# Bucketed attention, a gated feed-forward and routed experts on one core: a smaller set of sign projections, wider evictions and a new order of all lists

## The chip, the cores and the metric

The kernel runs on one core of one Trainium2 chip. The metric is the device time in microseconds (us) of one launch. The engines are named as the profile names them: PE is TensorE's matmul, PEld its weight load, DVE VectorE, ACT ScalarE, POOL GpSimd, SP the engine that issues most DMAs.

## What is computed

Three parts follow each other; the output of one is the input of the next, 768 tokens by 512.

```python
# 1. attention, 8 heads, 768 tokens, 64 wide; six sign bits put a token in a bucket
q_bits = (q @ proj) > 0 ; k_bits = (k @ proj) > 0          # proj: 64 x 6
mask   = bucket(q_bits)[:, None] == bucket(k_bits)[None, :]
scores = where(mask, q @ k.T / 8, -1e9)
attn   = exp(scores - max) ; attn /= attn.sum() + 1e-9
x      = attn @ v
# 2. gated feed-forward with a product over tokens
h      = gelu(x @ w_in)                                     # 512 -> 1024
u, v   = h[:, :512], h[:, 512:]
v_s    = w_sg @ (layernorm(v) * g_ln) + b_sg[:, None]       # 768 x 768 over tokens
x      = x + (u * v_s) @ w_out
# 3. eight experts; a token keeps the expert of the token before it when a gate says so
e      = sticky_argmax(x @ w_gate, x @ w_local)
out[s] = p[e] * (relu(x[s] @ w1[e]) @ w2[e])
```

## The kernel before

All matrices are split into a high part (fp32r) and a low part, and a product is the sum of high x high, high x low and low x high. The kernel is written as one program whose order on PE, DVE, ACT, POOL and SP is set by hand: four texts (`ATTENTION`, `FEED_FORWARD`, `MIXING`, `EXPERTS`) list steps such as `score 2 3` (head 2, tile 3), and each step issues its instructions on its engines in that order. An engine works through its own instructions in order and waits on semaphores for the others.

**Attention.** For each head h, `load_head` brings q and k (transposed, each twice, on partitions 0 to 63 and 64 to 127). `prep` makes the operands of 768 columns: k1 (high part of k), k2 (low part on partitions 0 to 63, key bits at 64 to 75), q1 (high part of q above, low part below), q2 (high part of q, query bits). `project` multiplies the sign projections into one PSUM bank for the keys and one for the queries, four matmuls each over two halves of 384 columns, eight a head (L404), and `bits` compares them with thresholds (L411, L413). `score` makes a tile of 128 x 768 scores in four matmuls (L420, L423), `row_max` reduces it on DVE (L427), `numerators` takes the exponential on ACT (L431), `turn` transposes three blocks of 128 x 128 on PE into a bank (L437), `evict` copies these 384 columns to SBUF on ACT (L443), `pv` multiplies them with the values (L453). `mean_part`, `to_x`, `sum_v` and the low parts of q and k use POOL. The operands of head h + 2 and the bits of head h + 1 are made while head h is scored.

**w_in and w_out** arrive as 64-bit floats and are taken apart on chip: `f64_chunks` is a generator, and each list step `conv` runs the next of its eight parts for a chunk of 128 x 512: a load on SP, a `lift` on ACT, four integer or scalar operations on DVE (L281 to L294), an addition on POOL (L273), a cast (L300), a subtraction on POOL (L273). Eight chunks are w_in's, four are w_out's; all twelve are converted beside attention.

**Feed-forward and mixing.** `hv` and `h` are the products with w_in (L314); for each token tile follow `sq`, `cub`, `tanh`, `gelu`, and for the half that is normalised `dev`, `z`, `var`, `norm`, `vh`, `vl`. `wsg` loads (L732), casts (ACT, L735) and splits (POOL, L737) a tile of w_sg, `mix` is the product over tokens (L744), `gated` and `gT` prepare its result, `out` is the product with w_out (L767), `res` adds x. PSUM buffers for `h`, `mix` and `out` come from a pool of four, taken in turn. `route` is a generator of some twenty small DVE steps for a token tile, with `what_all` (L868) among its last; its key goes through a transpose on PE (L822). `gx` and `fill` gather the tokens of the experts by matmul.

**Experts.** `wr` reads a quarter of one weight matrix of an expert (SP, L647), `wh` casts it (ACT, L655), `wl` splits off its low part (L661, on POOL for the parts in `ON_POOL`, else on DVE). `f`, `relu`, `ht`, `y` are an expert's two products, `yo` weighs the rows, `send` scatters them.

## Time and profile before

| | us | share of the span |
|---|---|---|
| median of 3 runs (346.26 to 347.0) | 346.53 | |
| the profiled execution | 347.04 | |
| its span, first to last instruction | 344.6 | |
| PE busy, 1860 matmuls | 327.5 | 95% |
| PEld busy, 1860 weight loads | 256.8 | 75% |
| DVE busy, 516 instructions | 272.5 | 79% |
| ACT busy, 432 | 233.9 | 68% |
| POOL busy, 162 | 203.5 | 59% |

The stages lie at about 0 to 12 us (start), 12 to 144 (attention), 144 to 178 (feed-forward and the first mixing products), 178 to 240 (mixing, output, routing), 240 to 338 (experts) and the end. Busy time is a sum over stages with different limits, and the end of a matmul is modelled in the profile; what a change is worth is read in its stage, from the steps between starts and from the waits.

### The profile page before, as it was taken

What the parts mean: (1) busy time and instruction counts of PE and PEld (TensorE: products, weight loads), DVE (VectorE), ACT (ScalarE), POOL (GpSimd) and SP (SyncE); (2) the same over time, 40 slices, a digit from 0 to 9 for tenths busy, and PEclk for the clock granted to TensorE, in tenths of its full rate; (3) what the DMA queues carried; (4) which work ended last, traced back from release to release, by engine and by line L of the source; (5) the groups of instructions that cost most, each with busy time, mean ns of one, the idle gap of its engine ahead of it and who ended that gap; (6) DMA issues with size and microseconds to landing.
All of it is one profiled execution on the core that took longest, in us unless ns stands there. A gap on an engine that the chain in (4) does not pass through costs nothing.

```text
span 344.6 us, 5450 instructions
## 1 busy us (share of the span) xinstructions
PE 327.5 (95%) x1860; PEld 256.8 (75%) x1860; DVE 272.5 (79%) x516; ACT 233.9 (68%) x432; POOL 203.5 (59%) x162
## 2 busy tenths in 40 slices
PE   7899999999999999999989999879999999999992
PEld 6787777667777657788767776559888888788892
DVE  4899999989998865788753768988589868798933
ACT  3589888888888775299455364364659786869540
POOL 3378867688858645247434674865732674574651
PEclk9999999999999999999999999998999999999997
DMA  6914043213421024011107429292979979999510
GB/s 248 331 45 153 3 152 121 92 38 119 133 82 61 10 62 132 0 57 52 46 7 253 124 89 327 81 357 66 343 252 303 336 288 368 348 330 364 216 60 32
DMA packets 25951, 55.82 MB, mean 162 GB/s; under 512 B 2878, under 2 KB 7486, under 8 KB 25920
## 3 DMA queue, kind: packets, MB, share of 16 engines
q1 hardware_dynamic: 23872, 50.67, 42.7%
q0 software_dynamic: 1120, 3.15, 2.7%
q10 hardware_dynamic: 928, 1.62, 1.4%
q8 instruction: 16, 0.26, 0.3%
q14 instruction: 15, 0.12, 0.1%
HBM read 52.28 MB, written 3.67 MB: 162 GB/s over the span
## 4 chain that ended last, share of the span: by engine, by line
PE 73%; DVE 13%; DMA 4%; ACT 4%; issue 2%; POOL 2%; SPq 0%; ACTq 0%; DVEq 0%; POOLq 0%
PE y L1045 10%; PE eh L1013 9%; PE t L437 9%; PE po L453 8%; PE s L420 5%; PE h L314 5%; PE s L423 5%; PE vs L744 5%; DMA raw<-in_w 3%; PE hv L314 3%; PE o L767 3%; PE pj L404 3%; PE gx L910 2%; PE hT L1024 1%; DVE what_all L868 1%
## 5 line engine op out<-in xcount | busy, mean ns | idle before, releaser
L661 POOL TENSOR_TENSOR w<-raw,w 128x1024 fp32r<-128x1024 f32 x23 | 58.6, 2549 | 40.3 <-ACT w L655 40.3
L655 ACT CAST w<-raw 128x1024 fp32r<-128x1024 f32 x64 | 65.3, 1052 | 12.7 <-DMA raw<-in_w 6.0
L661 DVE TENSOR_TENSOR w<-raw,w 128x1024 fp32r<-128x1024 f32 x41 | 59.9, 1492 | 5.1 <-ACT w L655 4.9
L443 ACT COPY pt<-t 128x384 f32<-128x384 f32 x96 | 43.4, 484 | 12.6 <-PE t L437 12.5
L431 ACT ACTIVATE e<-s,nb_all 128x768 f32<-128x768 f32 x48 | 43.6, 909 | 9.7 <-DVE nb_all L427 9.7
L427 DVE TENSOR_REDUCE nb_all<-s 128x1 f32<-128x768 f32 x48 | 45.4, 952 | 5.9 <-PE s L423 5.4
L437 PE MATMUL t<-ident,e 128*128 128x128 f32 x288 | 42.4, 274 | 0.0
L437 PEld LDWEIGHTS t<-ident,e 128*128 128x128 f32 x288 | 34.3, 140 | 8.6 <-ACT e L431 2.4
L453 PE MATMUL po<-pt,vt 128*64 128x384 f32 x192 | 35.4, 497 | 0.0
L1045 PE MATMUL y<-w,hh 128*128 128x512 f32 (+1 forms) x144 | 34.7, 374 | 0.3 <-ACT hh L1030 0.3
L420 PE MATMUL s<-k,q 128*128 128x384 f32 x96 | 28.5, 377 | 0.8 <-ACT e L431 0.7
L1045 PEld LDWEIGHTS y<-w,hh 128*128 128x128 f32 x144 | 24.4, 189 | 4.7 <-ACT hh L1030 0.8
L744 PE MATMUL vs<-vn,wshi 128*128 128x512 f32 x72 | 25.8, 406 | 1.4 <-ACT wshi L735 1.2
L423 PE MATMUL s<-k,q 76*128 76x384 f32 x96 | 25.1, 342 | 0.3 <-DVE q L411 0.3
L1013 PE MATMUL eh<-w,xh 128*128 128x512 f32 x96 | 25.0, 394 | 0.0
L392 POOL TENSOR_TENSOR k<-r,k 64x768 fp32r<-64x768 f32 x7 | 13.8, 1974 | 14.9 <-DVE k L382 9.5
L453 PEld LDWEIGHTS po<-pt,vt 128*64 128x64 f32 x192 | 12.0, 136 | 13.7 <-issue 13.4
L314 PE MATMUL h<-w_in_s,xTs 128*128 128x512 f32 x96 | 21.9, 389 | 0.0
L314 PEld LDWEIGHTS h<-w_in_s,xTs 128*128 128x128 f32 x96 | 18.0, 188 | 3.7
L1013 PEld LDWEIGHTS eh<-w,xh 128*128 128x128 f32 x96 | 17.7, 188 | 3.6
L420 PEld LDWEIGHTS s<-k,q 128*128 128x128 f32 x96 | 14.7, 190 | 7.2 <-ACT e L431 2.5
L1057 POOL DMA_INDIRECT out<-y,dst_row x8 | 12.3, 1532 | 11.2 <-ACT y L1054 4.7
(201 smaller groups left out, 738.4 us busy)
## 6 DMA issues: line engine op xcount, KB each, us to landing
raw<-in_w SPq DMA_DIRECT2D x64, 512.0 KB, 5.2
r<-in_qk SPq DMA_DIRECT2D x7, 768.0 KB, 4.4
raw<-in_w_in SPq DMA_DIRECT2D x8, 512.0 KB, 5.9
wsr<-in_w_sgT SPq DMA_DIRECT2D x6, 384.0 KB, 3.5
raw<-in_w_out SPq DMA_DIRECT2D x4, 512.0 KB, 3.5
vt<-in_v_tok ACTq DMA_DIRECT2D x1, 1536.0 KB, 9.3
xd<-x SPq DMA_DIRECT2D x6, 256.0 KB, 4.4
r<-in_qk SPq DMA_DIRECT2D x2, 384.0 KB, 4.0
```

Source lines behind the costliest of these rows:

```text
L314: nc.tensor.matmul(ps, a[:, kc, ts_], w_in_s[:, b, kc, ns], start=(kc == 0 and i == 0), stop=(kc == 3 and i == 2))
L420: nc.tensor.matmul(s[:, j, :HALF], q1[:, ts_], k1[:, j * HALF:(j + 1) * HALF], start=True, stop=False)
L427: nc.vector.tensor_reduce(nb_all[:, h, t:t + 1], ss[h, t][:, :, :HALF], axis=AX.XY, op=ALU.max, negate=True)
L431: nc.scalar.activation(e, ss.pop((h, t))[:, :, :HALF], AF.Exp, bias=nb_all[:, h, t:t + 1], accum_out=rs_all[:, h, t:t + 1])
L437: nc.tensor.transpose(ps[:, i * P:(i + 1) * P], es[h, t][:, g, i * P:(i + 1) * P], ident)
L443: nc.scalar.copy(dst, tps.pop((h, t, g))[:, :HALF].rearrange("p (i q) -> p i q", i=3))
L453: nc.tensor.matmul(po[j * D:(j + 1) * D, :HALF], vt[:, kt, h * D:(h + 1) * D], pt[j][:, kt, :], start=(kt == 0), stop=(kt == NT - 1))
L655: nc.scalar.copy(slabs_of[i, e][:, 0, q * 2:(q + 1) * 2, :], raws[part])
L661: eng.tensor_tensor(hl[:, 1, q * 2:(q + 1) * 2, :], raws.pop(part), hl[:, 0, q * 2:(q + 1) * 2, :].bitcast(F32), op=ALU.subtract)
L744: nc.tensor.matmul(ps, a[:, kc, :], b[:, kc, :], start=(k == 0), stop=(k == 17))
L1013: nc.tensor.matmul(ps[e, n], a[:, kc, :], slabs_of[1, e][:, b, kc * 2 + n, :], start=(k == 0), stop=(k == 11))
L1045: nc.tensor.matmul(yb[e][:, cs], a[:, kc, :], slabs_of[2, e][:, b, kc, cs], start=(k == 0), stop=(k == 23))
```

## The change

- The sign projections of a head use one bank of PSUM and three matmuls for each half of the columns, six a head in place of eight: a third operand, `b`, holds the high part of q above and the low part of k below. Head 0 keeps eight. For the other heads q1 is written by DVE, its high part is copied by two DMAs on SP to `b` and q2, and POOL writes the low part of k into `b`, from which a DMA copies it to k2. The ACT copy `hi` remains for head 0 alone, whose operands are made in halves; the load of head 0's q comes in two halves, k1 first.
- `turn` takes four blocks instead of three, `evict` copies 512 columns; the numerators lie in one tile, from which `pv` reads three runs of 128. The exponentials get four buffers in place of two, q and k two in place of a borrowed one.
- w_out is converted by a second generator, `cv`, in the feed-forward list (31 steps) and the mixing list (2), in buffers of those stages; its tile is allocated after attention.
- `on_pool` cuts POOL's long operations into two, three or four pieces. `ON_POOL` loses six weight splits, which go to DVE.
- All four lists are in a new order.

```diff
-ON_POOL |= {(i, e, 3) for i, e in W_ORDER[3:]}
+ON_POOL |= {(2, e, 3) for e in range(1, NE)}
+    def on_pool(out, a, b, op, n, axis=1):
+        size = out.shape[axis] // n
+        for i in range(n):
+            at = (slice(None),) * axis + (slice(i * size, (i + 1) * size),)
+            nc.gpsimd.tensor_tensor(out[at], a[at], b[at], op=op)
...
         def add_sub(c, i, out, x, y, op):
-            (nc.vector if (i, c) in ON_VECTOR else nc.gpsimd).tensor_tensor(out, x, y, op=op)
+            if (i, c) in on_vector:
+                nc.vector.tensor_tensor(out, x, y, op=op)
+            else:
+                on_pool(out, x, y, op, 2)
...
-            else:
-                r = ap1.tile([P, 2, S], F32, tag="r", name=f"r{h}", bufs=1)
+            r = ap1.tile([P, 2, S], F32, tag="r", name=f"r{h}", bufs=2)
             if h == 0:
                 nc.sync.dma_start(out=r[:, 1, :], in_=qk2[h, 1])
                 nc.scalar.dma_start(out=sm, in_=small)
-                nc.sync.dma_start(out=r[:, 0, :], in_=qk2[h, 0])
+                for g in range(2):
+                    nc.sync.dma_start(out=r[:, 0, g * HALF:(g + 1) * HALF], in_=qk2[h, 0][:, g * HALF:(g + 1) * HALF])
...
+            if what == "k1":
+                nc.vector.tensor_copy(k1, rk)
+            elif h == 0:
+                gs = slice(g * HALF, (g + 1) * HALF)
+                if what == "q2":
+                    nc.scalar.mul(q2[:, gs], rq[:, gs], QSC)
+                elif what == "hi":
+                    nc.scalar.mul(q1[0:D, gs], rq[0:D, gs], QSC)
+                elif what == "lo":
+                    nc.vector.scalar_tensor_tensor(q1[D:P, gs], rq[D:P, gs], QSC, q2[D:P, gs].bitcast(F32),
+                                                   op0=ALU.mult, op1=ALU.subtract)
...
             elif what == "q2":
-                nc.vector.tensor_scalar_mul(q2, rq, QSC)
+                b = ops[h, "b"]
+                nc.vector.tensor_scalar_mul(q1, rq, QSC)
+                nc.sync.dma_start(out=b[0:D].bitcast(F32), in_=q1[0:D].bitcast(F32))
+                nc.sync.dma_start(out=q2[0:D].bitcast(F32), in_=q1[0:D].bitcast(F32))
             elif what == "lo":
-                nc.gpsimd.tensor_scalar(rq[D:P], rq[D:P], QSC, 0.0, op0=ALU.mult, op1=ALU.add)
-                nc.gpsimd.tensor_tensor(q1[D:P], rq[D:P], q2[D:P].bitcast(F32), op=ALU.subtract)
+                for i in range(3):
+                    cs = slice(i * S // 3, (i + 1) * S // 3)
+                    nc.gpsimd.tensor_scalar(rq[D:P, cs], rq[D:P, cs], QSC, 0.0, op0=ALU.mult, op1=ALU.add)
+                    nc.gpsimd.tensor_tensor(q1[D:P, cs], rq[D:P, cs], q1[D:P, cs].bitcast(F32), op=ALU.subtract)
+            elif what == "k2":
+                b = ops[h, "b"]
+                on_pool(b[D:P], rk[D:P], k1[D:P].bitcast(F32), ALU.subtract, 3)
+                nc.sync.dma_start(out=k2[0:D].bitcast(F32), in_=b[D:P].bitcast(F32))
...
+            ps = sides[h, 0] = sides[h, 1] = bank("m", f"pj{h}")[0:ROWS, :HALF]
+            for g in range(2):
+                gs = slice(g * HALF, (g + 1) * HALF)
+                at = 32 - 32 * g
+                for n, (w_, m) in enumerate(((wz[:, 0, at:at + ROWS], k1), (wz[:, 1, at + 64:at + 64 + ROWS], q1),
+                                             (wb[:, at:at + ROWS], ops[h, "b"]))):
+                    nc.tensor.matmul(ps, w_, m[:, gs], start=(g == 0 and n == 0), stop=(g == 1 and n == 2))
...
-            e = es[h, t] = ap2.tile([P, 2, HALF], F32, tag="e", name=f"e{h}_{t}")
+            e = es[h, t] = ap2.tile([P, 2, HALF], F32, tag="e", name=f"e{h}_{t}", bufs=4)
...
-        def turn(h, t, g):
-            ps = tps[h, t, g] = bank("t", f"t{h}_{t}_{g}")
-            for i in range(3):
-                nc.tensor.transpose(ps[:, i * P:(i + 1) * P], es[h, t][:, g, i * P:(i + 1) * P], ident)
+        def turn(h, i):
+            ps = tps[h, i] = bank("t", f"t{h}_{i}")
+            for j in range(4):
+                t, k = divmod(4 * i + j, NT)
+                nc.tensor.transpose(ps[:, j * P:(j + 1) * P], es[h, t].rearrange("p g q -> p (g q)")[:, k * P:(k + 1) * P],
+                                    ident)
...
-            nc.scalar.copy(dst, tps.pop((h, t, g))[:, :HALF].rearrange("p (i q) -> p i q", i=3))
+            nc.scalar.copy(pts[h][:, 4 * i:4 * i + 4, :].rearrange("p b q -> p (b q)"), tps.pop((h, i)))
...
-                                     pt[j][:, kt, :], start=(kt == 0), stop=(kt == NT - 1))
+                                     pt.rearrange("p (t k) q -> p k t q", k=NT)[:, kt, j * 3:(j + 1) * 3, :],
+                                     start=(kt == 0), stop=(kt == NT - 1))
...
+        if part in ON_POOL:
+            for k in range(2):
+                on_pool(lo[:, k], raw[:, k], hi[:, k], ALU.subtract, 2)
+        else:
+            nc.vector.tensor_tensor(lo, raw, hi, op=ALU.subtract)
...
+        conv_out = f64_chunks(
+            [(w_out64[kc * P:(kc + 1) * P, :], w_out_s[:, 0, kc, :], w_out_s[:, 1, kc, :]) for kc in range(4)],
+            lambda: rawp.tile([P, 1024], U32, tag="raw", name="raw64"),
+            lambda: bp2.tile([P, DM], U32, tag="gh", name="cv_a"),
+            lambda: bp2.tile([P, DM], F32, tag="gl", name="cv_w"), ON_VECTOR2)
```

The feed-forward list's beginning, the mixing list's beginning and the experts' end, before and after:

```diff
-h 1 0, sq 1 0, cub 1 0, h 1 1, tanh 1 0, wsg 0 2, gelu 1 0, h 1 2, sq 1 1, h 1 3, sq 1 3, dev 1 0, cub 1 1,
+h 1 1, h 1 0, h 0 0, wsg 0 2, cv 0 0 *2, wsg 0 0, cv 0 0 *2, sq 1 1, cub 1 1, cv 0 0, wsg 0 1, sq 1 0, cv 0 0,
...
-mix 0 0, mix 0 1, mix 0 2, mix 1 0, mix 1 1, mix 0 3, mix 0 4, mix 0 5, mix 0 6, mix 1 2, mix 1 3, mix 0 7, mix 0 8,
+mix 1 0, wsg 2 2, mix 0 0, mix 0 1, mix 1 1, mix 0 2, mix 0 3, mix 0 4, mix 1 2, mix 0 5, mix 0 6, mix 1 3, mix 0 7,
...
-y 7 9, y 7 10, y 7 11, yo 7 1, yo 7 0, ext 0, send 7 0
+y 7 3, ht 7 1 2, y 7 4, y 7 5, send 6 0, y 7 6, y 7 7, y 7 8, yo 7 0, y 7 9, y 7 10, y 7 11, yo 7 1, ext 0, send 7 0
```

## Rows read from the trace of the kernel before

**Rows 1.** Stretches: busy us of PE, PEld, DVE, ACT, POOL, then clock, DMA.
```profile
12.00:144.00 132.00, 130.32 (x828) 96.24 (x829) 115.89 (x174) 105.61 (x235) 89.87 (x90) 1.00 0.28 92
144.00:178.00 34.00, 32.56 (x142) 25.96 (x141) 26.91 (x58) 25.25 (x49) 17.15 (x16) 1.00 0.12 39
...
207.00:240.00 33.00, 28.43 (x192) 22.88 (x191) 27.83 (x120) 15.60 (x32) 20.09 (x12) 0.95 0.63 215
240.00:330.00 90.00, 89.67 (x442) 74.01 (x440) 75.27 (x70) 68.22 (x88) 50.66 (x24) 1.00 0.87 303
```

**Rows 2.** Waits of PE over the whole span: total us, times, longest.
```profile
PE route_bank L822 <- DVE key L819: 3.0, 2, 1.6
...
PE vs L744 <- ACT wshi L735: 1.2, 1, 1.2
```

**Rows 3.** Timeline of PE in attention: start us, us, instructions.
```profile
61.25 0.87 PE L453 MATMUL po<-pt,vt 128*64 128x384 f32 x4
62.05 0.92 PE L404 MATMUL pj<-q,wz 128*66 128x384 f32 x4
62.80 0.51 PE L420 MATMUL s<-k,q 128*128 128x384 f32 x2
...
64.25 2.16 PE L453 MATMUL po<-pt,vt 128*64 128x384 f32 x12
66.34 0.62 PE L420 MATMUL s<-k,q 128*128 128x384 f32 x2
```

**Rows 4.** Lines by shape, copies out of PSUM: busy us, mean ns | idle.
```profile
L443 ACT COPY pt<-t 128x384 f32<-128x384 f32 x96 | 43.4, 484 | 12.6 <-PE t L437 12.5
...
L783 ACT COPY x2t<-x2T 128x512 f32<-128x512 f32 x6 | 3.5, 586 | 10.9 <-PE x2T L781 8.9 <-PE rk L851 2.0
```

**Rows 5.** Timeline of all engines at the start.
```profile
5.25 0.84 ACT L384 ACTIVATE q<-r 64x768 fp32r<-64x768 f32 x1 [2.79 <-DMA r<-in_qk]
...
7.87 1.24 DVE L413 TENSOR_SCALAR k<-pj,sm 12x384 fp32r<-12x384 f32 x2
...
10.52 0.96 DVE L427 TENSOR_REDUCE nb_all<-s 128x1 f32<-128x768 f32 x1 [0.77 <-PE s L423]
```

**Rows 6.** Lines: the 64-bit conversion, and the split of expert weights on DVE.
```profile
L661 DVE TENSOR_TENSOR w<-raw,w 128x1024 fp32r<-128x1024 f32 x41 | 59.9, 1492 | 5.1 <-ACT w L655 4.9
...
L273 POOL TENSOR_TENSOR cv_w<-cv_w,cv_a 128x512 f32<-128x512 f32 x11 | 14.3, 1300 | 7.3 <-DVE cv_w L285 7.2
...
L294 DVE SCALAR_TENSOR_TENSOR cv_w<-raw,cv_w 128x512 uint32<-128x512 uint32 x12 | 9.8, 816 | 2.3 <-POOL cv_w L273 2.1
...
L285 DVE SCALAR_TENSOR_TENSOR cv_w<-raw,cv_w 128x512 f32<-128x512 uint32 x12 | 9.4, 782 | 0.3
...
L281 DVE TENSOR_SCALAR cv_a<-cv_a 128x512 uint32<-128x512 uint32 x12 | 8.1, 674 | 0.0
...
L283 DVE TENSOR_SCALAR cv_w<-cv_a 128x512 uint32<-128x512 uint32 x12 | 5.9, 492 | 0.3
```

**Rows 7.** Timelines of DVE and of POOL in the feed-forward stage.
```profile
165.31 2.26 DVE L716 SCALAR_TENSOR_TENSOR z<-v,mu,gbc 128x512 f32<-128x512 f32 x1
...
165.17 1.85 POOL L737 TENSOR_TENSOR wslo<-wsr,wshi 128x768 fp32r<-128x768 f32 x1
```

**Rows 8.** Lines: `what_all`; then the timeline of DVE and POOL in routing.
```profile
L868 DVE TENSOR_SCALAR what_all<-oh_all,sm 128x8 f32<-128x8 f32 x6 | 6.1, 1010 | 0.0
...
216.22 0.22 DVE L846 TENSOR_SCALAR oh_all<-route_bank,rf 128x8 f32<-128x8 f32 x1
...
216.99 2.39 POOL L661 TENSOR_TENSOR w<-raw,w 128x1024 fp32r<-128x1024 f32 x1
...
217.85 1.56 DVE L868 TENSOR_SCALAR what_all<-oh_all,sm 128x8 f32<-128x8 f32 x1
```

**Rows 9.** DMA issues: KB of each, median us from issue to landing.
```profile
wsr<-in_w_sgT SPq DMA_DIRECT2D x6, 384.0 KB, 3.5
```

**Rows 10.** Chain of waits at the end of the span: start us, us.
```profile
337.81 0.85 ACT y L1054 x2
```

More of the change, by code (lines that the diff above doesn't have):

```diff
@@ new lines @@
+bits 2 0, prep 2 q2, exp 2 4, ev 2 5, sum 1 3, pv 1 2, turn 2 4, bits 2 3, score 3 0, conv 0, max 3 0, exp 2 5,
+score 3 1, max 3 1, prep 2 lo, turn 2 7, ev 2 4, mean 2, sum 3 0, sum 2 2, pv 1 3, fetch 3, pv 1 4, conv 0, ev 2 7,
+turn 2 8, conv 0 *2, exp 3 0, score 3 3, turn 2 6, pv 1 5, exp 3 1, prep 2 k1, ev 2 8, conv 0, sum 2 3, ev 2 6,
+prep 2 k2, max 3 3, out 2, fetch 4, exp 3 3, sum 3 1, to_x 2, score 3 2, turn 3 0, turn 3 1, mean 3, ev 3 0,
+max 3 2, to_x 3, score 3 4, ev 3 1, exp 3 2, conv 0, max 3 4, turn 3 2, turn 3 5, project 3, score 3 5, pv 2 0,
@@ new lines @@
+exp 5 3, conv 0, turn 5 2, score 5 5, ev 5 1, turn 5 3, pv 4 0, max 5 4, exp 5 4, bits 5 1, pv 4 1, ev 5 2,
+bits 5 0, ev 5 3, conv 0, pv 4 2, max 5 5, turn 5 5, turn 5 4, conv 0, sum 5 2, score 6 0, exp 5 5, bits 5 3,
+conv 0, ev 5 4, ev 5 5, conv 0, score 6 1, sum 6 0, sum 6 1, sum 5 3, turn 5 7, turn 5 6, conv 0, prep 5 q2, conv 0,
+pv 4 3, pv 4 4, max 6 0, ev 5 7, exp 6 0, prep 5 k1, prep 5 lo, ev 5 6, pv 4 5, max 6 1, conv 0, exp 6 1, prep 5 k2,
+score 6 2, xT 5, max 6 2, score 6 5, turn 5 8, conv 0, turn 6 1, conv 0, low 5, out 5, mean 6, pv 5 0, exp 6 2,
@@ L407, in bits @@
         def bits(h, i, g):
-            rows = slice(32 * g, 32 * g + NP)
-            src, dst = sides[h, i][rows, :HALF], ops[h][2 if i else 3][64:NB, g * HALF:(g + 1) * HALF]
+            at = 32 * g + (0 if i else 64)
+            rows = slice(at, at + NP)
+            src, dst = (late[g] if i and not h else sides[h, i])[rows, :HALF], ops[h][2 if i else 3][64:NB, g * HALF:(g + 1) * HALF]
             if i:
@@ L513 @@
                   for n in (1, 0) for kc in range(4)]
-        chunks += [(w_out64[kc * P:(kc + 1) * P, :], w_out_s[:, 0, kc, :], w_out_s[:, 1, kc, :])
-                   for kc in range(4)]
         warm = bank("v", "warm")
```

356 lines of the change are left out of this document (182 added, 174 removed).

## The prediction

> **What bounds the kernel now.** I read four views in this order: the table of stretches, the waits of TensorE (PE), the timeline of PE, and the lines with their means. The stretches [rows 1] show PE busy for 130.32 of 132 us in attention (12 to 144 us), 32.56 of 34 in the feed-forward stage, 28.43 of 33 in the routing stretch (207 to 240), 89.67 of 90 in the experts. A busy PE may still be a slow one, so the second look is at single steps: in attention each group of matmuls starts where the group before it ends [rows 3], with no releaser named. The waits that PE does have are few [rows 2]: 3.0 us in two waits for the routing key, 1.2 us for a cast weight tile at the start of mixing. So a TensorE instruction removed in attention should be worth its step; work added to VectorE (DVE) or ScalarE costs only where it makes PE wait; and the routing stretch is a chain, not a stream.
>
> The profiled execution took 347.04 us (span 344.6, 2.4 outside it); the median of the runs is 346.53. I add changes up against 347.04 and then take the same difference off the median. This measurement can tell 0.2% (0.7 us) from no change.
>
> **Part 1: six projections a head.** Head 0 keeps its eight (four for the keys, twice two for the queries); the seven others go from eight to six, 64 to 50 in all. Four of them take from 62.05 to 62.80, where the next group starts [rows 3]: 0.19 us each. 14 x 0.19 = **-2.6 us**, on the path since PE is the stream there. The wider result (108 rows for 66) changes no column count; I cost it at nothing.
> What it needs in return: ScalarE loses the copy `hi`, 0.84 us at head 0's size [rows 5], seven times, 5.9 us; that engine is off the path (105.61 of 132 busy [rows 1]), so nothing for that. SP gains three copies a head inside the chip's buffer, 192 KB each, 21 in all. No row shows such a copy; the nearest is a load of 384 KB that lands 3.5 us after issue [rows 9]. I take 3.5 us and call it hidden: a head lasts (144 - 12) / 8 = 16.5 us and its operands are prepared a head ahead. The copies wait on SP's queue for DVE (q1) and for GpSimd (POOL) (the lower part of k); behind them stand the load of the next 64-bit chunk, whose `lift` ScalarE waits for in order, and the next head's q and k. If the cover is gone, each head's first score waits up to 3.5 us, so the bounds are 0 and +24; nearest is 0, because the copies are half the size of the row's load and have a head's time. The cover is weakest for head 1, prepared while the kernel starts.
>
> **Part 2: evictions of 512 columns.** The 288 transposes stay. Evictions go from 96 x 0.484 us to 72 of a shape that another line copies in 0.586 us [rows 4]: 46.5 to 42.2 us on ScalarE, off the path: 0. The P x V product now reads its moving side in three runs of 128 columns instead of 384 in one; no row shows a matmul with runs so far apart. Bounds: 0, as evictions that write in three runs (0.484) and in one (0.586 for a third more) differ by width alone, and +5% of those matmuls' time, 96 pairs x 0.32 us = 31 us, so +1.5. I take 0.
> The list of attention has 17 separate runs of P x V where the old one has 20. A run of two steps takes 0.80 us and one of six 2.09 [rows 3]; so a step is (2.09 - 0.80) / 4 = 0.32 and a run has 0.80 - 2 x 0.32 = 0.16 us of its own. 3 x 0.16 = **-0.5 us**.
>
> **Part 3: the start.** Now ScalarE makes `hi` over all 768 columns from 5.25 us, then q2; DVE has both key bits from 7.87 ahead of the query bits; the first row maximum starts at 10.52 [rows 5]. In the new program q comes in two halves, `hi`, q2 and `lo` work on halves, and the first score needs one half of the query bits. Taking q2 and `lo`, of the same 768 columns, at the 0.84 us of `hi`, half of three such operations leaves the chain to the first score: 3 x 0.42 = **-1.3 us**. Bounds: 0 (DVE's k2 and key bits stand in that place) and -2 (one key bit of 0.61 us, half of the row's 1.24, goes too).
>
> **Part 4: w_out converted later.** A chunk has four DVE operations of means 0.674, 0.492, 0.782 and 0.816 us and two POOL ones of 1.3 [rows 6]; four chunks are 11.1 us on DVE and 10.4 on POOL. In attention they hid beneath PE, where DVE is busy 115.89 of 132 us; their going frees DVE but not PE: 0. In the new list of the feed-forward 31 of 33 conversion steps stand between its operations. There DVE has 26.91 us of 34 [rows 1]: 26.9 + 11.1 = 38.0, 4.0 more than the stretch holds, even if DVE never idles. What is late: the first mixing products need the GpSimd and DVE halves of all six normalised tiles, one product takes a PSUM buffer that the gelu of an h tile must first free (it stands behind 24 conversion steps), and the first cast of mixing's third weight tile on ScalarE stands behind a copy that follows DVE's last gelu, the wait of 1.2 us of [rows 2]. Against it stands Part 5 here: one `z` took 2.26 us because POOL's operation of 1.85 us from 165.17 to 167.02 held it [rows 7]; in thirds that wait is at most 0.6, so about 1 us comes back. I take 4.0 - 1.0 = **+3.0 us**. Bounds: 0 (DVE's work falls ahead of what PE needs, behind the long h products) and +11 (DVE's idle is not usable).
>
> **Part 5: POOL in pieces.** In routing, `what_all`, 128 x 8, took 1.56 us from 217.85 to 219.41, where the split on POOL from 216.99 ended (219.38); a DVE operation of the same shape took 0.22 [rows 8]. All six take 1.01 on the mean: 6 x (1.01 - 0.22) = 4.7 us, and they stand in front of the key, for which PE waited 3.0 us [rows 2]. With a split in four pieces of about 0.6 us the rest of a piece is 0.3 on the mean, so about 3 us of DVE time comes back; with what is not on the path I take **-2.5 us**, bounds 0 (the new order may put other waits there) and -5 (both key waits go, and the slow clock too: the granted clock of the stretch is 0.95 [rows 1], which is 2.4 GHz but for (1 - 0.95) x 2 x 33 = 3.3 us at 1.2 GHz; at full rate these would be half). POOL pays a start for each piece: 512 elements take 1300 ns [rows 6], 1024 take 2390 [rows 8], so 2 x 1300 - 2390 = 210 ns a cut; of about 150 cuts some 70 lie in attention, 15 us on an engine that is busy 89.87 of 132 us there [rows 1]: 0. Six more weight splits go to DVE in the experts, 1.49 us each [rows 6]: its 75.27 us of 90 [rows 1] become 84.2, still under PE's: 0, at worst +2.
>
> **Part 6: the end.** After the last matmul two half rows are weighed in 0.85 us [rows 10]; the new list weighs the first half during the last matmuls: **-0.4 us**. The rest of the reordered lists I cannot cost by rows: 0, with the range.
>
> Sum: -2.6 - 0.5 - 1.3 + 3.0 - 2.5 - 0.4 = -4.3 us: 347.04 becomes 342.7, and the median **342.2 us**.
>
> [...]
>
> **The rivals.**
> A. The forecast, 342.2 (own range 339 to 345): chance 0.50.
> B. Better: the feed-forward takes the conversion under its h products (0 for +3.0) and routing loses 4.5 us instead of 2.5: 342.2 - 3.0 - 2.0 = 337.2. For it: DVE is idle for 34 - 26.9 = 7.1 us of that stretch. Against: the list has most conversion steps ahead of the last normalised tile. Chance 0.19.
> C. Attention is not bound by PE's steps but by DVE (88% busy) and the row maxima; removed projections leave gaps. Then -2.6 and -0.5 fall away: 345.3. Against: no releaser between PE's groups. Chance 0.10, half of it within 0.2%.
> D. Slower: DVE becomes the bound of the feed-forward. If z, gelu and conversion steps queue in order behind POOL's ever-present pieces, DVE's 7 us of idle cannot be used and all 11.1 us are added: 342.2 + 8.1 = 350.3. It decides from a loss of 3.0 + 4.3 = 7.3 us in that stage. For it: DVE is in order and POOL gets 10.4 us more there. Chance 0.14.
> E. The copies inside the buffer come late: 1 us a head for seven heads: 349.2. Chance 0.07.
>
> **The numbers.** Faster by over 0.2%: A 0.50, B 0.19, half of C 0.05: 0.74. Within: C's other part and the edge of D: 0.07. Slower: the rest of D and E: 0.19. The range 336 to 349 leaves out B's far end and most of D.
>
> **What would show it.** Right: PE's sum over the projection line falls by a fifth to 50 instructions; the first row maximum starts near 9.2 us; attention's last matmul some 4.5 us earlier; then some 3 us lost before the third mixing tile, with PE waiting for DVE's gelu or ScalarE's cast; `what_all` at some 0.4 us and key waits under 2 us; one half row after the last matmul. Wrong: PE waits on k2, q2 or the copies inside attention (E); steps of P x V longer than 0.32 us; DVE above 34 us of work before mixing's first product with PE idle for over 7 us (D); or attention as long as before with gaps (C).

## The result and the profile after

The changed kernel takes 348.52 us (347.92 to 348.99), the kernel before 346.54 (346.26 to 347.0): ratio 1.0055, 95% interval 1.0036 to 1.0074. It is slower by half a per cent; the forecast was 342.2 us. Executions over 1.5% slower than the fastest of their kernel, three of b_pieces and one of a_fix_dup, are left out of the times and ratios below; the trace of b_pieces is of one of them, and is longer than that of the kernel before in the experts alone (104.0 us for 99.7). The profiled execution took 347.92 us, span 346.1 (before: 347.04 and 344.6).

Four landmarks that both traces have, the first product of mixing (`vs`), the first of the experts (`eh`), the products `pc` behind the last expert and the end of the span, tell where:

| stretch | before, us | after, us | difference | forecast |
|---|---|---|---|---|
| start and attention, to the first `vs` | 168.66 | 167.93 | -0.73 | -4.4 |
| mixing and routing, `vs` to `eh` | 70.30 | 71.48 | +1.18 | +0.5 |
| experts, `eh` to `pc` | 99.74 | 99.39 | -0.35 | -0.4 |
| end, `pc` to the end of the span | 5.94 | 7.35 | +1.41 | 0 |
| span | 344.64 | 346.15 | +1.51 | -4.3 |

The stretches of the changed kernel, columns as in [rows 1]:

```profile
12.00:144.00 132.00, 128.95 (x820) 96.53 (x818) 107.78 (x160) 96.63 (x199) 95.07 (x157) 1.00 0.42 124
144.00:178.00 34.00, 32.68 (x140) 25.59 (x138) 32.81 (x70) 25.43 (x50) 30.95 (x38) 1.00 0.24 85
207.00:240.00 33.00, 28.55 (x194) 22.61 (x193) 27.44 (x122) 15.81 (x34) 24.47 (x36) 0.95 0.55 175
240.00:330.00 90.00, 90.00 (x439) 74.41 (x438) 71.89 (x79) 68.73 (x89) 37.68 (x38) 1.00 0.89 312
```

Against [rows 1], VectorE is 8 us and ScalarE 9 us freer in attention, but PE's busy time there has fallen by only 1.4 us: what PE does not compute, it now waits. In the feed-forward (second row) VectorE went from 26.91 to 32.81 us and GpSimd from 17.15 to 30.95, and PE still has its 32.7 us. PE's waits over the span, columns as in [rows 2]:

```profile
PE route_bank L878 <- DVE what_all L928: 3.1, 1, 3.1
PE vs L800 <- ACT wshi L791: 1.9, 1, 1.9
...
PE pj L440 <- DMA b<-q: 1.3, 1, 1.3
PE pj_None L431 <- DVE k L395: 0.9, 1, 0.9
...
PE s L459 <- DVE q L447: 0.7, 1, 0.7
...
PE pj L440 <- POOL q L405: 0.5, 1, 0.5
```

The two old waits are still there, as long as before or longer. The projections have new ones: for a copy inside the buffer (`b<-q`) and for GpSimd.

**The routing wait.** First GpSimd's, then VectorE's timeline (start us, us, instruction, times):

```profile
209.19 1.44 POOL L215 TENSOR_TENSOR x2l<-x,x2h 128x256 fp32r<-128x256 f32 x2
210.57 2.79 POOL L215 TENSOR_TENSOR w<-raw,w 128x256 fp32r<-128x256 f32 x4
...
209.90 3.49 DVE L924 TENSOR_SCALAR what_all<-oh_all,sm 128x8 f32<-128x8 f32 x1
213.30 0.15 DVE L858 TENSOR_REDUCE rmx<-lg 128x1 f32<-128x8 f32 x1
```

The tiny operation that [rows 8] showed at 1.56 us beside a whole split now runs 3.49 us, through five pieces issued back to back (the second of `x2l`, then four of `w`), and ends 0.03 us after the last of them. The chance to get in at each cut, on which Part 5 rested, was not taken once.

**The feed-forward wait.** ScalarE's timeline, then VectorE's:

```profile
177.87 0.38 ACT L988 COPY route_bank<-cst 128x256 f32<-128x256 f32 x1 [4.53 <-DVE route_bank L987]
178.19 0.83 ACT L791 CAST wshi<-wsr 128x768 fp32r<-128x768 f32 x1
...
174.97 1.87 DVE L764 SCALAR_TENSOR_TENSOR u<-sq,h 128x512 f32<-128x512 f32 x3
177.07 0.69 DVE L297 SCALAR_TENSOR_TENSOR cv_w<-raw,cv_w 128x512 uint32<-128x512 uint32 x1 [0.23 <-POOL cv_w L215]
177.68 0.16 DVE L987 COPY route_bank<-sm 128x8 f32<-128x8 f32 x1
```

ScalarE stands 4.53 us for a copy of 0.16 us that is queued on VectorE behind gelus and conversion steps, and the cast that mixing needs stands behind ScalarE.

**The end.** Branch instructions of the `If` around the extra tiles on PE's sequencer (times, then ns min/median/max, start us); the first row is of the changed kernel, the second of the one before:

```profile
L1161 PEldq COMPARE_BRANCH  x1: 3593/3593/3593, 341.4 to 341.4; - x1
```
```profile
L1096 PEldq COMPARE_BRANCH  x1: 465/465/465, 341.3 to 341.3; - x1
```

Nothing of this kind stood in the forecast. In both traces a DMA queue of the kind `instruction` moves 16 KB once every 180 to 330 PE instructions up to the last product; I take these for the blocks of PE's code. Before, the last block was brought at 335.97 us, 38 instructions ahead of the branch; after, the last was brought at 318.61, and the next only at 342.44, while PE stood at the branch.

### The profile page after: what moved, and what is told of

The parts are those of the page before. It is cut to its first block, busy times and chain, and to the rows that moved or that the text cites. A ratio compares the mean times of both kernels' runs of the same rounds, so it can differ in the third digit from the quotient of the medians.

```text
span 346.1 us, 5609 instructions
## 1 busy us (share of the span) xinstructions
PE 324.5 (94%) x1842; PEld 255.1 (74%) x1842; DVE 267.1 (77%) x524; ACT 228.1 (66%) x403; POOL 216.4 (63%) x314
## 3 DMA queue, kind: packets, MB, share of 16 engines
HBM read 52.28 MB, written 3.67 MB: 162 GB/s over the span
## 4 chain that ended last, share of the span: by engine, by line
PE 68%; DVE 18%; POOL 5%; issue 3%; DMA 3%; ACT 1%; POOLq 0%; DVEq 0%; ACTq 0%
PE y L1110 13%; PE eh L1078 13%; PE po L490 7%; PE vs L800 7%; PE t L474 6%; PE o L823 4%; PE s L456 3%; PE s L459 3%; PE hv L317 3%; DVE nb_all L463 2%; PE hT L1089 2%; DMA b<-q 2%; DVE q L447 1%; PE pj L440 1%; POOL b L215 1%
## 5 line engine op out<-in xcount | busy, mean ns | idle before, releaser
L215 POOL TENSOR_TENSOR w<-raw,w 128x256 fp32r<-128x256 f32 x68 | 50.7, 779 | 36.0 <-ACT w L708 36.0
L718 DVE TENSOR_TENSOR w<-raw,w 128x1024 fp32r<-128x1024 f32 x47 | 57.2, 1257 | 4.6 <-ACT w L708 4.6
L467 ACT ACTIVATE e<-s,nb_all 128x768 f32<-128x768 f32 x48 | 43.5, 907 | 17.5 <-DVE nb_all L463 16.1
L480 ACT COPY pt<-t 128x512 f32<-128x512 f32 x72 | 40.3, 588 | 11.7 <-PE t L474 11.3
L474 PE MATMUL t<-ident,e 128*128 128x128 f32 x288 | 39.8, 274 | 0.4 <-ACT pt L480 0.2
L490 PE MATMUL po<-pt,vt 128*64 128x384 f32 x192 | 34.7, 495 | 0.0
L1110 PE MATMUL y<-w,hh 128*128 128x512 f32 (+1 forms) x144 | 33.5, 371 | 0.6 <-ACT y L1119 0.6
L1122 POOL DMA_INDIRECT out<-y,dst_row x8 | 11.2, 1399 | 23.9 <-DVE y L1117 11.3
L215 POOL TENSOR_TENSOR b<-r,k 64x256 fp32r<-64x256 f32 x21 | 15.9, 780 | 10.0 <-DVE k L384 10.0
L215 POOL TENSOR_TENSOR cv_w<-cv_w,cv_a 128x256 f32<-128x256 f32 x24 | 17.8, 763 | 2.9 <-PE hv L317 2.0
## 6 DMA issues: line engine op xcount, KB each, us to landing
vt<-in_v_tok ACTq DMA_DIRECT2D x1, 1536.0 KB, 12.1
```

The lines of the kernel that those rows point to most:

```text
L215: nc.gpsimd.tensor_tensor(out[at], a[at], b[at], op=op)
L467: nc.scalar.activation(e, ss.pop((h, t))[:, :, :HALF], AF.Exp, bias=nb_all[:, h, t:t + 1], accum_out=rs_all[:, h, t:t + 1])
L474: nc.tensor.transpose(ps[:, j * P:(j + 1) * P], es[h, t].rearrange("p g q -> p (g q)")[:, k * P:(k + 1) * P], ident)
L480: nc.scalar.copy(pts[h][:, 4 * i:4 * i + 4, :].rearrange("p b q -> p (b q)"), tps.pop((h, i)))
L490: nc.tensor.matmul(po[j * D:(j + 1) * D, :HALF], vt[:, kt, h * D:(h + 1) * D], pt.rearrange("p (t k) q -> p k t q", k=NT)[:, kt, j * 3:(j ...
L718: nc.vector.tensor_tensor(lo, raw, hi, op=ALU.subtract)
```

## The experiments

All times are medians, beside runs of the kernel before on the same chip; the ratio to that kernel carries the comparison. The expectations say "head 1" for the head whose copies are issued at 23.2 us; in the kernel's own count that is head 2, the second of the seven with copies.

**The code at the end.** Idle matmuls on the changed kernel, and fewer on the kernel before.

```diff
+            idle = bank("t", "idle")[:, :NE]
+            for _ in range(24):
+                nc.tensor.matmul(idle, ones_b, ohb_all[:, 0, :], start=True, stop=True)
             pc = bank("v", "pc")[:, :NE]
```

> The changed kernel plus 24 idle matmuls of 8 columns ahead of the product pc that ends the experts, 48 more instructions on PE than the changed kernel, 15 more than the kernel before. Theory (code): the branch at the end took 3.59 us after and 0.46 us before, because the last block of PE's code was brought at 318.6 us after and at 336.0 us before, and the block behind the branch only once the branch stood there; with the count of instructions back above that of before, the branch takes about 0.5 us again, and the kernel is 1 to 1.5 us shorter than the changed one, some 347.1 us. Rival: the 3.59 us are a wait for the last write or for a value (they began where DVE's last operation ended), nothing to do with where the code lies; then the branch stays at 3 to 4 us and the time at 348.5 us or up to 1 us more for the idle matmuls.

347.42 us, ratio 1.0027 (1.0008 to 1.0045), where the change alone has 1.0055: 1.0 us shorter by the ratios with more instructions. The two intervals overlap a little; in the traces the end is 1.4 us shorter.

```diff
-... warm 0 12, ... warm 0 10, ...      (list ATTENTION of the kernel before)
```

> The kernel before, without two groups of idle matmuls in attention (22 matmuls, 44 instructions on PE fewer; the change had 33 fewer). Theory (code): the block of PE's code that was brought at 336.0 us stood 38 instructions ahead of the branch; with 44 fewer it is no longer brought ahead, the branch at the end takes 3 to 4 us in place of 0.46 us, and the kernel is about 1.4 us longer, 347.5 to 348 us, but for what the missing idle matmuls do to the start. Rival (the change's long branch has to do with its last writes or with its extra tiles' order, not with the count): the branch stays at 0.5 us and the end is as before.

347.19 us, ratio 1.0021 (1.0008 to 1.0035): longer with less work. The branch rows, a_pad first:

```profile
L1164 PEldq COMPARE_BRANCH  x1: 460/460/460, 341.6 to 341.6; - x1
```
```profile
L1096 PEldq COMPARE_BRANCH  x1: 3573/3573/3573, 340.2 to 340.2; - x1
```

Shown: the long branch follows the count of PE's instructions, in either kernel, and not what the change computes. From `pc` to the end the span takes 5.9 to 6.0 us where the branch is short: before and b_fix (branch at PE instruction 3785), a_pad, a_fix and a_fix_dup2 (3800). It takes 7.3 to 7.4 us where it is long: after (3752), b_less_pe (3741), a_fix_dup (3828). In these three the next block was brought 1.0 us after the branch had begun, and the branch ended 2.6 us behind that; where it is short, the next block came only after the branch had ended. In a_fix_dup a block had been brought 66 instructions ahead of the branch, and it was long all the same; so the distance to the last block alone doesn't decide. Where the code behind the branch lies may count too; no run settles that. What the branch does in that time no trace shows; from 0.46 to 3.59 us it took 3.1 us more, and the end 1.4 us more.

**The id column in routing.**

```diff
-nc.vector.tensor_scalar(what_all[:, t, 0, :], oh, tok_1[:, t:t + 1], None, op0=ALU.mult)
+nc.vector.tensor_scalar(what_all[:, t, 0, :], rev_p, f, tok_1[:, t:t + 1], op0=ALU.is_equal, op1=ALU.mult)
```

> The changed kernel, with the one operation of routing that forms the id column (128x8) read from the token's rank in PSUM and not from the one-hot row in SBUF; same count of operations. Theory (port): this operation ran 3.49 us in the changed kernel, against a median of 0.29 us for its five sisters, because it asked for GpSimd's turn at SBUF and got none between five pieces issued back to back; with only one operand read from SBUF it needs no such turn, runs in 0.2 to 0.4 us, PE's wait of 3.1 us in routing goes, and the kernel is 2 to 3 us shorter, 345.5 to 346.5 us. Rival: the operation only stood for whatever DVE does then, and the next operation of DVE's with two operands in SBUF waits through the same pieces: PE's wait moves by one operation and the time stays within 0.5 us of 348.5 us.

344.93 us, ratio 0.9949 (0.993 to 0.9967): 3.7 us under the changed kernel by the ratios, more than expected. In the traces `vs` to `eh` is 4.7 us shorter (66.8 for 71.5). The six operations, in a_psum_id and then in the changed kernel (ns min/median/max):

```profile
L924 DVE TENSOR_SCALAR what_all<-route_bank,rf,sm x6: 275/277/278, 201.3 to 233.6; 128x8 f32<-128x8 f32 x6
```
```profile
L924 DVE TENSOR_SCALAR what_all<-oh_all,sm x6: 222/258/3491, 201.2 to 238.2; 128x8 f32<-128x8 f32 x6
```

With the wide operand in PSUM none of the six took over 278 ns. The rest of the gain, beside the 3.1 us of the wait, I put down to the clock. Stretches of the changed kernel, then of a_psum_id:

```profile
211.00:215.00 4.00, 0.94 (x6) 0.47 (x5) 3.96 (x10) 1.13 (x4) 2.36 (x4) 1.00 0.49 201
215.00:220.00 5.00, 5.00 (x21) 3.69 (x19) 3.52 (x17) 2.79 (x5) 4.18 (x6) 0.66 0.01 2
```
```profile
211.00:215.00 4.00, 4.00 (x24) 2.97 (x22) 3.67 (x17) 3.70 (x8) 4.00 (x7) 1.00 0.51 203
215.00:220.00 5.00, 5.00 (x32) 3.63 (x31) 4.32 (x19) 2.64 (x6) 5.00 (x8) 1.00 0.51 116
```

Behind the wait the granted clock was 0.66 over 5 us: 0.50 from 215.87 us on for (1 - 0.66) x 2 x 5 = 3.4 us, and 1.00 else. Two steps of 512 columns in that time (217.56 and 217.99 us) took 0.43 us each, where the median over the trace is 0.23. With PE at half its rate the 3.4 us cost 1.7 us, an estimate. Without the wait the granted clock was 1.00 over the same 5 us, and PE went through 32 matmuls instead of 21.
The operation still reads two columns of one value per partition (`rf`, `sm`) from SBUF. The rows show that it took up to 3.49 us, to the end of GpSimd's fifth piece, with its wide operand in SBUF, and at most 0.28 us with it in PSUM; that a turn at SBUF is what it waited for, as the theory has it, no row shows.

**Pieces or whole operations.** Three runs: the split of expert weights in four pieces on the kernel before (b_pieces), that split whole on the changed kernel (a_w_whole), and all of GpSimd's long operations whole on the changed kernel (a_whole).

```diff
 # b_pieces, on the kernel before
+            for k in range(4):
+                cs = slice(k % 2 * 256, (k % 2 + 1) * 256)
+                nc.gpsimd.tensor_tensor(lo[:, k // 2, cs], raw[:, k // 2, cs], hi[:, k // 2, cs], op=ALU.subtract)
 # a_w_whole and a_whole, on the changed kernel
-            for k in range(2):
-                on_pool(lo[:, k], raw[:, k], hi[:, k], ALU.subtract, 2)
+            nc.gpsimd.tensor_tensor(lo, raw, hi, op=ALU.subtract)
 # a_whole besides
     def on_pool(out, a, b, op, n, axis=1):
+        n = 1
```

> The kernel before, with GpSimd's share of the expert weights' split in four pieces each and nothing else. The forecast gave this part 2.5 us: 344 us. Theory after the runs so far: whether the id column's operation gets its turn depends on whether pieces stand back to back when it asks; each split is then 3.0 us in place of 2.5 us, and an operation kept out through all pieces waits longer than before, so the kernel is no faster, 346.5 to 349 us. Rival (as forecast): the turn passes at each cut, the four waits of 0.66 to 1.69 us fall to 0.3 us each, and PE's 3.0 us wait for the routing table falls with them.

> The changed kernel, with GpSimd's share of the expert weights' split whole (128x1024) and its other pieces kept. The kernel with all operations whole was 6 us slower than the changed one, most of it (5.2 us) ahead of the feed-forward. Theory: that is attention's pieces, in an order laid out for them; the split in pieces brings routing nothing, the id column waits 0.7 to 2.2 us for one or two whole splits as in the kernel before, and the time is 347.5 to 349 us. Rival (the forecast's part 5): whole splits cost routing 2.5 us, 350.5 us or above.

> The changed kernel with GpSimd's long operations whole again, all else as changed (part 5 undone). The forecast gave the pieces 2.5 us: by it the kernel would be 351 us. Theory after the runs so far: an id column's operation that meets one whole split waits for its rest only (0.7 to 1.7 us in the kernel before), where in pieces it was kept out through five of them (3.3 us); so the routing loses no more than it does in pieces, GpSimd saves some 0.23 us a cut, other operations of VectorE's in attention and feed-forward wait longer, and the time is within 1 us of 348.5 us. Rival: whole operations hold wslo and the id columns up in several blocks, 350 us or above.

b_pieces: 346.95 us, ratio 0.9994 (0.9965 to 1.0023), no difference. a_w_whole: 347.77 us, 1.0041 (1.0015 to 1.0066), against 1.0055 in pieces: no difference either. In the routing stretch the pieces of Part 5 are worth nothing, in either kernel. b_pieces shows the same kind of wait, GpSimd's row first:

```profile
223.18 3.50 POOL L664 TENSOR_TENSOR w<-raw,w 128x256 fp32r<-128x256 f32 x5
...
224.57 2.13 DVE L872 TENSOR_SCALAR what_all<-oh_all,sm 128x8 f32<-128x8 f32 x1
```

It began 0.02 us after a piece (224.55) and was kept out through three, until the last of the row ended at 226.67; the case of 3.49 us began 0.02 us after a piece too, and came again in a_pad, a_rev_act and a_vt_first. Others got in at the next cut, with a piece right behind: one in b_pieces that began 0.15 us after a piece, one in a_vt_late (a run further below) 0.06 us after. But a_vt_late also has one that began 0.23 us after a piece of the first row and was kept out through five:

```profile
216.39 2.84 POOL L215 TENSOR_TENSOR x2l<-x,x2h 128x256 fp32r<-128x256 f32 x4
219.15 2.84 POOL L215 TENSOR_TENSOR w<-raw,w 128x256 fp32r<-128x256 f32 x4
...
218.69 3.33 DVE L924 TENSOR_SCALAR what_all<-oh_all,sm 128x8 f32<-128x8 f32 x1
```

In all three the wait ended with the last piece of the row. The moment of asking does not sort these cases, and what decides is open.

a_whole: 354.61 us, 1.022 (1.0177 to 1.0263): 5.7 us slower than in pieces by the ratios, so my theory of 1 us fell, and its rival was right about the size. It was wrong about most of the place: of the 6.8 us between the two traces 5.2 come ahead of the first `vs` (171.74 us from PE's first instruction, for 166.57) and 1.8 between `vs` and `eh`. Ahead of `vs` VectorE's operations that overlap one of GpSimd's ran 17.5 us over the fastest of their line and shape, for 12.0, and 1.9 us is one stall of PE for which the trace names nothing. The sum alone does not make PE late: the kernel before has 15.2 with its first `vs` at 167.30. So pieces do pay in attention in this order, which the forecast had at 0; but the order of the lists was laid out for pieces, and how whole operations would do in an order of their own is open.

**The copy of the reversed ranks.**

```diff
-nc.vector.tensor_copy(rev_p, revc)
+nc.scalar.copy(rev_p, revc)
```

> The changed kernel, with the copy of the reversed ranks (rev_p) on ScalarE in place of VectorE. Theory: ScalarE stood 4.53 us for this copy of VectorE's at 177.7 us, and PE then waited 2.1 us for ScalarE's wshi; with the copy on ScalarE that wait falls to under 1 us and the kernel is 1 to 2 us shorter, 346.5 to 347.5 us. Rival: VectorE's gelu operations, not the copy, set the time of the second mixing half: PE's wait in the feed-forward stays at about 2.7 us in sum and the time within 0.3 us of 348.5 us.

346.86 us, ratio 1.0005 (0.9984 to 1.0025): 1.7 us under the changed kernel, as expected. PE's longest waits in it:

```profile
PE route_bank L878 <- DVE what_all L928: 3.0, 1, 3.0
PE warm L562 <- POOL ident masks.py:199: 1.4, 1, 1.4
PE pj_None L431 <- DVE k L395: 0.9, 1, 0.9
```

The wait for `wshi` has left the list. Not the gelus held mixing up, but ScalarE's place in a queue. The gain is that of the medians; the profiled execution (347.69 us, of 344.71 to 347.98) loses it again. At the late id column it is 1.2 us ahead of the changed kernel (208.71 for 209.90); behind the wait the granted clock is 0.69 from 211 to 215 us and 0.56 from 215 to 220, which is 6.9 us at 0.50 for 3.4, and the next id column stands at 221.30 for 221.32.

**Both edits in the kernel before, and all three in the changed one.** b_fix has the id column and the copy; a_fix has these and the idle matmuls.

```diff
+nc.vector.tensor_scalar(what_all[:, t, 0, :], rev_p, f, tok_1[:, t:t + 1], op0=ALU.is_equal, op1=ALU.mult)
+nc.scalar.copy(rev_p, revc)
+for _ in range(24): nc.tensor.matmul(idle, ...)      (a_fix alone)
```

> The kernel before, with both small edits of routing and feed-forward alone: the id column formed from the ranks in PSUM, and the copy of the reversed ranks on ScalarE. Theory (port): here the id column's operations waited 0.66, 1.69, 1.34 and 1.05 us for GpSimd's split of expert weights to end, and PE waited 3.0 us for the routing table; these waits go and the kernel is 2 to 4 us shorter, 342.5 to 344.5 us. Then what the edit gains in the changed kernel is not the change's own gain: both kernels lose by the same operation, and the pieces did not free it. Rival: in the kernel before, one whole split ends the wait in time, something else is late next, and the time stays within 0.7 us of 346.5 us.

> The changed kernel with three edits: idle matmuls ahead of pc, id column from PSUM, copy of the reversed ranks on ScalarE. Theory: the three losses stand one behind the other on PE's path, so the gains add up: -1 (end), -3.5 (routing) and -1.5 (feed-forward), 342 to 343 us. Rival: ScalarE's earlier wshi only brings the wait to the next operand (GpSimd's wslo or the layer norm), and the sum is that of two edits, 343.5 to 344.5 us.

b_fix: 341.07 us, 0.9839 (0.9818 to 0.9859). a_fix: 340.75 us, 0.9836 (0.9815 to 0.9856). Both are faster than expected. a_fix is 7.6 us under the changed kernel by the ratios, 1.2 more than the three edits gave singly (1.0, 3.7 and 1.7); what the trace of a_rev_act lost to the clock behind the routing wait may be part of that. These beat both kernels, by 1.6% of the one before, and they are equal. So the two edits gain nothing that belongs to the change, and the change with its three accidents mended is worth nothing that can be measured. In a_fix the granted clock is 1.00 from 207 to 240 us, where the changed kernel has 0.95:

```profile
207.00:240.00 33.00, 31.56 (x216) 25.60 (x208) 29.18 (x125) 18.70 (x36) 25.98 (x36) 1.00 0.68 222
```

**The copies beside the big load.** Three places for the load of the values (`vt 0`, 1.5 MB) in the list of attention: first, a few entries later than in the change, and, on a_fix, behind head 0's last numerators.

```diff
-prep -1 k1, score 0 1, ... bits 0 2, vt 0, max 0 4, ... prep 0 q2, exp 0 5, ... exp 0 4, score 1 2
+vt 0, prep -1 k1, ...          (a_vt_first)
+... prep 0 q2, vt 0, exp 0 5   (a_vt_late)
+... exp 0 4, vt 0, score 1 2   (a_fix_vt)
```

> The changed kernel, with the load of the values' weights (1.5 MB) issued first of the list for attention, as early as before the change or earlier. Theory: head 1's copy of the query bits landed 6.8 us after its issue, beside that load, where later copies land in 2.5 to 2.6 us, and PE waited 1.3 us for it and 3.07 us for the operands of heads 1 and 2 in all; with the load early these waits fall by 0.5 to 1.5 us and the kernel is that much shorter, 347 to 348 us; GpSimd's pieces of the same bits end next. Rival: the loads of q and k that the first scores wait for now share the queues with the big one, and the start loses 1 us or more: 349 us or above.

> The changed kernel, with the load of the values' weights issued after head 1's copy of the query bits (at about 23.5 us, not 16.75 us). Theory (crowding): that copy landed 6.8 us after its issue beside the 1.5 MB load; alone it lands in 2.5 to 3.5 us, PE's wait of 1.3 to 1.5 us for it goes to under 0.5 us, and the kernel is 0.5 to 1.3 us shorter, 347.2 to 348 us. Rival: the values then land after 33.7 us, where the first product with them stood, and PE waits there instead: no gain, or 1 to 2 us lost.

> The changed kernel with the three edits (idle matmuls ahead of pc, id column from PSUM, reversed ranks on ScalarE), and the load of the values' weights issued at about 25 us, behind head 1's copies and its load of r. The run in which the load was moved by one numerator's place left its issue at 16.75 us, so it is moved past one more. Theory (crowding): head 1's copy lands in 2.5 to 4 us in place of 6.8 us, PE's waits for head 1's operands fall by 0.4 to 1.3 us (GpSimd's pieces of the same bits end at 29.6 us, the copy landed at 30.0 us), and the kernel is that much shorter than with the three edits alone (340.75 us): 339.5 to 340.4 us. Rival: the values land after 35 us, the first products with them, at 33.3 us, wait 2 us or more, and it is slower: 341.5 us or above.

In the changed kernel the load is issued at 16.75 us and lands 12.1 us later; the copy `b<-q` issued at 23.20 lands at 30.00, after 6.8 us, where those from 44.7 to 64 us took 2.5 to 2.6. a_vt_first: 349.94 us, 1.0095 (1.0075 to 1.0114): issued at 11.11, the load lies on the copies of the head before (5.9 us and more), and PE waits 2.3 us for one of them. The copy `b<-q` of the kernel's head 2, issued at 25.43 when the load has landed (19.07), then takes 2.6 us. a_vt_late: 349.01 us, 1.0052 (1.0022 to 1.0081); the load was still issued at 16.75, so this run is a repeat of the changed kernel and settles nothing else. a_fix_vt: 343.17 us, 0.9902 (0.9862 to 0.9941), 2.4 us slower than a_fix: the load went out at 21.99, not at 25, right ahead of the copies, which landed after 7.1 and 8.4 us. The values landed at 32.01, so the slower time is not the rival's late values. That copies beside the load are late is shown three times; in a_fix_vt the copy issued at 16.27, behind the 768 KB load of the next q and k (15.77), took 5.7 us too, before the big load was issued. That the change would gain without it is not: GpSimd's pieces of the same bits end next.

```profile
27.47 2.10 POOL L215 TENSOR_TENSOR b<-r,k 64x256 fp32r<-64x256 f32 x3
```

They end at 29.57, 0.43 us ahead of the copy.

**What a projection product is worth.** a_fix with the 14 products put back, as repeats; first with 24 idle matmuls at the end, then with 10, so that the branch stands at instruction 3800 as in a_fix (run again beside it).

```diff
             ps = sides[h, 0] = sides[h, 1] = bank("m", f"pj{h}")[0:ROWS, :HALF]
+            for g in range(2):
+                nc.tensor.matmul(ps, wz[:, 0, 32 - 32 * g:32 - 32 * g + ROWS], k1[:, g * HALF:(g + 1) * HALF], start=True, stop=True)
```

> The changed kernel with the three edits, and two projection products more for each of heads 1 to 7 (14 in all, as many as the change took away; each is done twice, the result is the same). Theory (attention is bound by PE, the first part of the forecast): each costs its step of 0.19 us, the products begin the feed-forward 2.6 us later, and the kernel takes 343.0 to 343.6 us. Rival (another engine binds attention, as in the forecast's rival C): the 2.6 us vanish in waits that stand there anyway, and the time stays within 0.7 us of 340.75 us.

> The changed kernel with the three edits once more, beside the next run on one chip: 340.5 to 341.3 us, by every theory.

> As the run with 14 projection products more, but with 10 idle matmuls ahead of pc in place of 24, so that the branch stands at the same count of PE instructions (3800) as without the products; there the branch took 3.67 us again and added 1.4 us of its own. The trace of that run had 2.4 us more of PE's steps ahead of the feed-forward and 1.3 us less of waits, so that the feed-forward began 1.04 us later. Theory (the waits for heads 1 and 2 absorb a part): 1 to 1.4 us above the kernel with the three edits, 341.7 to 342.3 us; then 14 products fewer are worth 1 us in this order, not the 2.6 us of the forecast. Rival (attention is bound by PE throughout): 2.4 us or more above it, 343 us.

a_fix_dup: 343.54 us, 0.9915 (0.9875 to 0.9956), with a branch of 3.67 us again, so this number holds the long branch's 1.4 us. a_fix_again: 341.2 us, 0.9851 (0.9827 to 0.9874). a_fix_dup2: 341.48 us, 0.9885 (0.9846 to 0.9924): 0.3 us more by the medians, 1.2 by the ratios, whose intervals overlap.

The traces go nearer. The list up to the first `vs` is the same in all four kernels but for the repeats, and the start is not: the first score begins at 8.29 us in a_fix, 9.00 in a_fix_again, 8.35 in a_fix_dup and 8.21 in a_fix_dup2. From there to the first `vs` it takes 159.7 us without the repeats, in both traces, and 160.7 and 160.8 with them. Set beside a_fix score by score, the repeats of heads 1 and 2 shift nothing; those of heads 3, 4 and 5 each shift all that follows by 0.3 us, nearly their 2 x 0.19; those of heads 6 and 7 shift a few scores by 0.4 us, and then no more. Attention in a_fix_again, then in a_fix_dup2:

```profile
12.00:144.00 132.00, 129.10 (x821) 96.37 (x819) 107.67 (x160) 97.46 (x199) 95.41 (x157) 1.00 0.42 124
```
```profile
12.00:144.00 132.00, 129.72 (x829) 98.29 (x828) 106.73 (x158) 96.42 (x199) 95.44 (x157) 1.00 0.42 124
```

The products of the first and the last heads fill time in which PE stood. Of 14 x 0.19 = 2.7 us 1.0 to 1.1 reach the first `vs`. The rival that PE binds throughout (2.4 us) falls; in heads 3 to 5 PE does bind.

## Why the forecast was wrong

The forecast was right about the work that was removed and wrong about waits: it took new ones for hidden, old ones for gone, and had no row for the one at the end. PE's steps and waits below are sums up to the first `vs` over the starts of neighbouring PE instructions: what lies over 0.1 us above the median for such a pair and has a releaser is a wait, the rest is steps.

- **Part 1, the projections (-2.6 forecast).** The steps on them fell from 12.34 to 9.98 us, -2.4, as worked out. But all of PE's waits together rose from 4.1 to 6.4 us. The step that failed is "a TensorE instruction removed in attention should be worth its step": it was read from back-to-back starts in one head in the middle [rows 3], where it holds, while the first heads' products wait for operands. By the repeats the 14 products are worth 1.0 to 1.1 us, 0.07 to 0.08 each on the mean, not 0.19. The bounds on the copies were right to name the start as weakest, and rival E's mechanism came there alone (1.3 us in one wait), not in seven heads. That "its operands are prepared a head ahead" does not hold for the first two heads with copies. Rival C, an attention that PE's steps do not bind, came true in that part, though not by VectorE's load: that engine is busy 107.78 of 132 us. By the first of the two rows above PE was 97.8% busy there, and it had room for 1.6 of 2.7 us all the same.
- **Part 2 (-0.5).** Right: the steps of P x V fell by 0.51 us (34.04 to 33.53), and reading three runs costs nothing, 495 ns on the mean for 497:

```profile
L490 PE MATMUL po<-pt,vt 128*64 128x384 f32 x192 | 34.7, 495 | 0.0
...
L480 ACT COPY pt<-t 128x512 f32<-128x512 f32 x72 | 40.3, 588 | 11.7 <-PE t L474 11.3
```

- **Part 3, the start (-1.3).** Wrong at the bound that it named, VectorE. In VectorE's timeline the key's `k2` and both key bits still stand ahead of the first query bits:

```profile
5.93 0.94 DVE L395 TENSOR_TENSOR k<-r,k 64x768 fp32r<-64x768 f32 x1
...
7.70 1.25 DVE L449 TENSOR_SCALAR k<-pj_None,sm 12x384 fp32r<-12x384 f32 x2 [0.24 <-PE pj_None L431]
8.99 0.61 DVE L447 TENSOR_SCALAR q<-pj,sm 12x384 fp32r<-12x384 f32 x1
...
10.31 0.96 DVE L463 TENSOR_REDUCE nb_all<-s 128x1 f32<-128x768 f32 x1
```

The first row maximum starts at 10.31 for 10.52 [rows 5]: 0.2 us. Halving ScalarE's operations shortened a chain that was not the last.
- **Part 4, the conversion (+3.0).** The place was right to the line: ScalarE's cast of the third weight tile behind a copy that follows VectorE's last gelu. The size was not: 1.9 us for 1.2, with 0.4 for `wslo`, some +1 us in all. VectorE gained 5.9 us in the stretch, not 11.1, and PE's long products covered it. And it was no cost of the conversion: one copy on another engine takes 1.7 us off. The step from VectorE's sum of work to PE's lateness (38.0 us in a stretch of 34) is what failed, and rival D with it.
- **Part 5, the pieces (-2.5).** The failed step is "the rest of a piece is 0.3 on the mean": operations were kept out through three and five pieces. Five of the six operations did get short (median 0.26 us for 1.08 before), but the sixth took the whole wait, and behind it the granted clock was 0.50 for 3.4 us (from 215.87 us), as it had been in the kernel before (from 231.34 us). The traces give the clock as a share; the forecast's 2.4 and 1.2 GHz are in them columns a ns: 384 in a median step of 0.161 us of P x V at a granted clock of 1.00, and 512 in each of two steps of 0.43 us at 0.50. Pieces alone gave 0.9994. In attention, costed at 0, they carry up to 5 us in this order. The six splits that VectorE took over in the experts cost nothing, as forecast, but not as sized: its busy time there went from 75.27 to 71.89 us and not to 84.2, since a split took 1.26 us on the mean for 1.51.
- **Part 6 (-0.4).** Right: one half row of 0.47 us is left after the last product, and the experts' stretch is 0.35 us shorter, though that stretch differs by more between executions of one list (98.9 to 99.8 us with the old).
- **Not in the forecast: +1.4** at the end, from 33 PE instructions fewer, among them the 28 of Part 1 (14 products with their weight loads).

So of a forecast of -4.3, -4.4 was to come by the first `vs` and -0.7 came. Even that stands at the first score already (8.32 us for 9.00), and the first score differs by as much between executions of one list (8.65 to 9.22 us with the old, 8.21 to 9.00 with the new); from there to the first `vs` both kernels take 159.6 to 159.7 us, so the new waits took up what the steps gave. That mixing and routing came within 0.7 us of the forecast is luck: +3.0 came as some +1, and -2.5 did not come. The range reached 349 and holds the time; the sign was wrong, since each term was priced as if its neighbour's queue would stay as it was.

## What to carry to other kernels

An instruction taken off the engine that seems to bind is worth its step only where that engine's operands are early: count the waits at the first and last turn of a loop, not at one turn in its middle. Before an operation is cut into pieces to let another engine in, look whether that engine's operation can read its wide operand from PSUM instead; here, in routing, that gave 3.7 us and the cuts none. And after any change in the count of instructions look at the branches: a branch that took 3.59 us in place of 0.46, with 33 PE instructions fewer ahead of it, made the end 1.4 us longer here, more than any of the planned gains was seen to give.
